# Attention and top-2 experts on one core: the first expert's tokens transposed on TensorE, gating cut at each hand-over, first weights split on GpSimd, zero fills issued by ScalarE

## The chip, the cores and the metric

One core of a Trainium2 chip runs the whole program. The metric is device time in microseconds (us) of that one core, as the median of several runs. A profile of one further execution shows what each engine did: TensorE (PE, with its weight loads PEld), VectorE (DVE), ScalarE (ACT), GpSimd (POOL) and the issuing engine SyncE (SP).

## What is computed

Linear attention without a softmax, a norm for each head, and then a layer of eight experts of which each token uses two. Cut to what matters:

```python
kv  = einsum('bhsd,bhse->bhde', k, v)          # 8 batches, 8 heads, 576 tokens, width 64
out = einsum('bhsd,bhde->bhse', q, kv)
x   = out / sqrt(mean(out*out, -1) + 1e-6) * g_norm      # 4608 tokens x 512
noisy = x @ w_gate + log1p(exp(x @ w_noise)) * noise
top2  = the two largest of 8;  weight = softmax over the two
for e in range(8):                             # w1[e] 512x1024, w2[e] 1024x512
    for k in range(2):
        m = top2[:, k] == e
        y[m] += weight[m, k] * (relu(x[m] @ w1[e]) @ w2[e])
```

## The kernel before

**Two stages that overlap.** The front stage computes 36 tiles of 128 tokens, nine for every two batches. `prep(b)` makes the 64x64 matrices of a batch (PE L539, then copies and small products by ACT L544, PE L549, ACT L552, PE L558, ACT L561, all through the tile `kvt` and into `kvw`). `tile_mm` multiplies the queries of one tile with it (PE L571, into the tile `big`). `advance(t)` is a hand-written pipeline: ACT copies `big` into `o` (L579, two `big` buffers), every second tile ACT squares it (`sq`, L586), DVE sums (`ss`, L588), ACT takes Ln and Exp of that sum one tile later (L592, L593), POOL scales tokens and logits one tile after that (`lg`, `x`, L602 and L606), DVE sums the logits (`zl`, L611), and ACT's queue writes the tokens to DRAM (`xs`, L615). Every engine takes its instructions in the order in which the program emits them: an instruction that waits holds all behind it on that engine.

**Gating in four chunks.** After tiles 10, 18, 28 and 36 a chunk is routed: `gating` turns logits into a choice of two experts and their weights, on DVE, ACT (L139, L140, L154) and POOL (L142, L143, L167) in turn, and PE counts the choices (L174). `onehots` and `place` (L302 to L315) make the list of an expert's tokens, and `finish` (L323) reads it out. These are generators: `yield n` gives the front stage n turns of `pump` before they go on; `pump` is called three times for each tile.

**Experts in units.** Expert 0 has five units of two tiles of tokens, here called units 0 to 4; the other experts have units of four, four and two. A unit's tokens are fetched by an indirect DMA on POOL's queue (`gather`, L357, tile `xg`), cut into a high and a low f16 half by ACT and POOL (`halves`, L364 and L365, tile `xh`), transposed by DMA (`xpose`, L377, tile `xT`; ACT's queue issues it for units 0 to 2, SP's for all others), multiplied by the first weights (`l1`, PE L416, relu by ACT L421 and DVE L422 into `hT`), by the second (`l2`, PE L460, ACT L481 into `y`), and added into the output by an indirect DMA that accumulates (`scatter`, POOL L394). Units 0, 1 and 2 are ready before the front stage ends: `fill_early` gives PE one piece of them per tile, so that l1 of unit 0 stands between the last tiles. The rest of unit 0 and units 1 and 2 follow the last tile.

**Weights.** Each expert's weights are scaled and cut into f16 halves. For expert 0 (`first_weights`, two steps per tile) DVE makes the low half straight from the f32 weights (L255, L257) while ACT makes the high one (L253).

**Zero fill.** The output has to be zero before the first scatter. Six DMAs of 1536 KB each (`clear`, L385) on SP's queue do that, emitted at tiles 30 to 35. The first scatter waits for all six.

Of the kernel before, what the change touches and what calls it, by code (L numbers as in the profile page):

```python
# [31 lines left out]
CHUNKS = (10, 18, 28, 36)  # L32
SL, W1 = 2, 2
KT, KV2 = 14, 0
XW, PY = 2, 5
LAG = 2
KC, KR, KQ, KX, KO = 5, 1, 4, 3, 3
GY = 5
WY, YH = 4, 4
YG, YX = 7, 7  # L40
KW0, KW1, KW = 100, 10, 8
MARKS = {10: 2, 18: 4, 28: 6}
EARLY = len(MARKS)
# [8 lines left out]
def attention_moe(ctx: ExitStack, tc: tile.TileContext, kvm, kvr, qt, gn, wgn, noise, w1, w2, out):  # L52
# [79 lines left out]
    def gating(a, b):  # L132
        n = b - a
        s = slice(a, b)
        w = rout.tile([P, n, E], F32, name="gt_w", bufs=2)
        nl = rout.tile([P, n, E], F32, name="gt_nl", bufs=2)
        V.scalar_tensor_tensor(w, zl[:, s, 8:16], -1.0, zl[:, s, 8:16], op0=OP.mult, op1=OP.max)
        V.tensor_scalar(nl, zl[:, s, 8:16], 1.0 / XS, 0.0, op0=OP.mult, op1=OP.max)
        A.activation(w, w, AF.Exp, scale=1.0 / XS)  # L139
        A.activation(w, w, AF.Ln, bias=1.0)  # L140
        yield 1
        G.tensor_tensor(w, w, nl, OP.add)  # L142
        G.tensor_tensor(w, w, nz[:, s], OP.mult)  # L143
        yield 1
        V.scalar_tensor_tensor(nl, zl[:, s, 0:8], 1.0 / XS, w, op0=OP.mult, op1=OP.add)
        mx = rout.tile([P, n, 8], F32, name="gt_mx", bufs=2)
        ix = rout.tile([P, n, 8], U32, name="gt_ix", bufs=2)
        for i in range(n):
            V.max(mx[:, i], nl[:, i])
        for i in range(n):  # L150
            V.max_index(ix[:, i], mx[:, i], nl[:, i])
        d = rout.tile([P, n, 4], F32, name="gt_d", bufs=2)
        V.tensor_tensor(d[:, :, 0:1], mx[:, :, 1:2], mx[:, :, 0:1], OP.subtract)
        A.activation(d[:, :, 1:2], d[:, :, 0:1], AF.Exp)  # L154
        ixf = rout.tile([P, n, 2], F32, name="gt_ixf", bufs=2)
        V.tensor_copy(ixf, ix[:, :, 0:2])
        yield 1
        oh = rout.tile([P, 2, n, E], F32, name="gt_oh", bufs=1)
        j8 = jf[:, None, 0:E].to_broadcast([P, n, E])
        for k in range(2):  # L160
            V.tensor_tensor(oh[:, k], j8, ixf[:, :, k:k + 1].to_broadcast([P, n, E]), OP.is_equal)
        V.tensor_scalar(d[:, :, 2:3], d[:, :, 1:2], 1.0, 1e-9, op0=OP.add, op1=OP.add)
        sel = rout.tile([P, n, E], BF, name="gt_sel", bufs=2)
        V.tensor_tensor(sel, oh[:, 0], oh[:, 1], OP.add)
        V.reciprocal(d[:, :, 2:3], d[:, :, 2:3])
        yield 1
        G.tensor_tensor(d[:, :, 3:4], d[:, :, 1:2], d[:, :, 2:3], OP.mult)  # L167
        for k in range(2):
            G.tensor_tensor(oh[:, k], oh[:, k], d[:, :, 2 + k:3 + k].to_broadcast([P, n, E]), OP.mult)
        G.tensor_tensor(ge[:, s], oh[:, 0], oh[:, 1], OP.add)  # L170
        yield GY
        for i in range(n):
            m = NT - a - i
            T.matmul(R[:, a + i + 1:, :], ones, sel[:, i:i + 1, :].to_broadcast([P, m, E]),  # L174
                     start=False, stop=False, skip_group_check=True)
        T.matmul(R[:, s, :], before, sel, start=False, stop=True, skip_group_check=True)
        V.tensor_copy(vals[:, 2, s], ge[:, s])
        yield 1
        vi = rout.tile([P, 2, n, E], I32, name="gt_vi", bufs=1)
        V.scalar_tensor_tensor(vi[:, 0], sel, -OFF, R[:, s, :], op0=OP.mult, op1=OP.add)  # L180
        G.tensor_tensor(w, ge[:, s], vals[:, 2, s], OP.subtract)
        if a:
            V.tensor_scalar(vi[:, 0, :, 0:1], vi[:, 0, :, 0:1], corr, None, op0=OP.add)
        if b in MARKS:
            gap = rout.tile([P, 1], F32, name="gap")
            V.tensor_tensor(gap, R[:, b, 0:1], corr, OP.add)
            V.tensor_scalar(gap, gap, -1.0, float(MARKS[b] * P), op0=OP.mult, op1=OP.add)
            V.tensor_scalar(gap, gap, 0.0, None, op0=OP.max)
            V.tensor_tensor(corr, corr, gap, OP.add)
        V.tensor_scalar(vi[:, 1], vi[:, 0], P - 1, None, op0=OP.bitwise_and)  # L190
        V.tensor_copy(lnb[:, s], vi[:, 1])
        V.tensor_tensor(t128[:, s], vi[:, 0], vi[:, 1], OP.subtract)
        yield 1
        V.tensor_copy(vals[:, 3, s], w)
        G.tensor_tensor(vals[:, 4, s], w, vals[:, 3, s], OP.subtract)
        yield 1
# [99 lines left out]
    def onehots(e, a, b):  # L296
        s = slice(a, b)
        n = b - a
        oa = lists.tile([P, n, P], BF, name="oa")
        ot = lists.tile([P, n, CAP], BF, name="ot")  # L300
        ob = lists.tile([P, n, 5, CAP], BF, name="ob")
        V.tensor_tensor(oa, jb[:, None, :].to_broadcast([P, n, P]),  # L302
                        lnb[:, s, e:e + 1].to_broadcast([P, n, P]), OP.is_equal)
        yield 1
        V.tensor_tensor(ot, tb10[:, None, :].to_broadcast([P, n, CAP]),
                        t128[:, s, e:e + 1].to_broadcast([P, n, CAP]), OP.is_equal)
        V.tensor_tensor(ob, ot[:, :, None, :].to_broadcast([P, n, 5, CAP]),
                        vals[:, :, s, e:e + 1].rearrange("p v n o -> p n v o").to_broadcast([P, n, 5, CAP]), OP.mult)
        return oa, ob
# [58 lines left out]
    def xpose(u):  # L368
        e, tiles, tail = units[u]
        if u < EARLY:  # L370
            if not u:
                late["xT"] = moe_a.tile([P, 8, 512], F16, name="xT")
            x = late["xT"][:, :, u % 2 * 256:(u % 2 + 1) * 256]
        else:
            x = (moe_a if (u - EARLY) % 2 else late["moe"]).tile([P, 8, 512], F16, name="xT")
        for i, t in enumerate(tiles):
            (A if u < EARLY else SP).dma_start_transpose(x[:, :, i * P:(i + 1) * P], XG[u, t])  # L377
        XT[u] = x

    outs = deque()  # L380
    zeroed = []
    ov = out[CAP * P:].rearrange("(p r) d -> p r d", p=P)

    def clear(r, n):
        zeroed.append(SP.dma_start(ov[:, r:r + n], zrow[:, None, :].to_broadcast([P, n, DM])).ins)  # L385

    tick = rout.tile([1, 1], F32, name="tick")
    SC = {e: [] for e in range(-1, E)}
# [99 lines left out]
    def drain(gen):  # L488
        for _ in gen:
            pass  # L490

    def moe_early(u):
        while "c" not in WT[0]:
            yield 1
        finish(0, M0, slice(2 * u, 2 * u + 2))
        yield 1
        gather(u)
        yield YG
        halves(u)
        yield YH  # L500
        xpose(u)
        yield YX
        while 0 not in loaded:
            yield 1
        early.extend([l1(u), l2(u)])

    early = deque()
# [3 lines left out]
    with tc.tile_pool(name="p1", bufs=2) as p1, tc.tile_pool(name="ps1", bufs=1, space=PSUM) as ps1:  # L511
# [148 lines left out]
        def fill_early():  # L660
            while early:
                try:
                    next(early[0])
                    if front[0] >= NT:
                        scatter()
                    return
                except StopIteration:
                    early.popleft()

        def first_weights():  # L670
            yield from weights(0, wts_a, V, SL)
            loaded.add(0)

        w0 = first_weights()
# [10 lines left out]
        for b in range(B):  # L685
# [7 lines left out]
            for args in per[b]:  # L693
                t = front[0] = args[0]
                tile_mm(*args)
                keep_warm(KW if t < KT else KV2)
                next(steps, None)
                if args[1] + args[4] < P:
                    next(steps, None)
                    continue  # L700
                pump()
                advance(t)
                next(steps, None)
                if t - LAG in CHUNKS:
                    side.append([1, chunk(CHUNKS.index(t - LAG))])
                pump()
                if t >= W1:
                    next(w0, None)
                    next(w0, None)
                fill_early()  # L710
                pump()
                if t >= NT - 6:
                    clear(6 * (t - NT + 6), 6)
            drain(steps)
        for t in range(NT, NT + 4):
            front[0] = t
# [3 lines left out]
                side.append([1, chunk(CHUNKS.index(t - LAG))])  # L720
            pump()
            fill_early()
    drain(w0)
    after = ExitStack()
    late["moe"] = after.enter_context(tc.tile_pool(name="moe_b", bufs=1))
# [4 lines left out]
    late["ps"] = ctx.enter_context(tc.tile_pool(name="psb", bufs=4, space=PSUM))  # L730
    psl = ctx.enter_context(tc.tile_pool(name="psl", bufs=1, space=PSUM))
    bg = deque()
    AHEAD = {0: gather, 8: halves, 15: xpose}
    hold = [0]

    def prepare(e):
# [55 lines left out]
    for u in (EARLY, EARLY + 1)[:1 + (GB > 4)]:  # L792
        for _ in range(XW):
            fill_early()
            fill()
        halves(u)
        fill_early()
        xpose(u)
    while early:
        fill_early()  # L800
        for _ in range(FE):
# [1 line left out]
    for u in range(EARLY, len(units) + 1):  # L803
        if u < len(units):
# [14 lines left out]
            if tiles[0] == 0 and e + 1 < E:  # L819
                bg.append(locate(e + 1))  # L820
                bg.append(prepare(e + 1))
            todo = deque([halves, xpose] if u + 1 < len(units) and u + 1 not in XT else ())
            while tail and todo:
                fill()
                todo.popleft()(u + 1)
# [94 lines left out]
```

## Time and profile before

| What | Value |
|---|---|
| Median of 3 runs | 981.3 us (980.8 to 986.57) |
| The profiled execution | 986.19 us, of which the span from first to last instruction is 984.3 us |
| PE busy | 906.2 us, 92% of the span |
| DVE, ACT, POOL busy | 460.2, 318.4, 380.9 us |
| PE busy from 0 to 50, 50 to 100, 100 to 150, 150 to 200 us | 46.17, 36.28, 35.54, 39.17 us |
| Granted PE clock in those four | 0.95, 0.74, 0.80, 0.90 |

Times within the profile count from the start of the span. A row of the timeline gives start, duration, engine, line, operation and tiles, and in brackets how long the engine had been idle before it and what ended that. The granted clock is the share of full speed at which the throttle let TensorE run.

### The profile page before, as it was taken

The numbers are of one execution on the slowest core, as the hardware profiler recorded it, in microseconds if no ns is written. First come the engines' busy times: TensorE is split into PE (matmuls) and PEld (weight loads), VectorE is DVE, ScalarE is ACT, GpSimd is POOL, SyncE is SP. The second block draws the span as 40 slices with busy tenths as digits, with TensorE's granted clock in tenths as the row PEclk, the third lists the DMA queues.
The fourth block names the chain that finished last, engine by engine and source line by source line (L and its number), as shares of the span: only waits on it lengthen the run. The fifth ranks groups of instructions, "written<-read, shape, count | busy, mean of one in ns | idle before, by whom it ended". The sixth has DMA issues, their size and how long they took to land.

```text
span 984.3 us, 15681 instructions
## 1 busy us (share of the span) xinstructions
PE 906.2 (92%) x6356; PEld 508.8 (52%) x6356; DVE 460.2 (47%) x933; ACT 318.4 (32%) x511; POOL 380.9 (39%) x414
## 2 busy tenths in 40 slices
PE   9986585999999999999999999999999989999994
PEld 8875473567444544464445344464444434644452
DVE  1678465555747343823563355534373456211110
ACT  1564343224334231323232332333243224222111
POOL 0445453554533352334244144325334553142122
PEclk9985697999999999999999899999999999999998
DMA  8998899655854873476259454637258644462224
GB/s 329 340 390 342 182 392 290 174 108 87 253 97 99 146 172 57 99 158 155 61 107 172 109 108 109 142 85 161 44 143 162 147 105 58 48 114 45 44 37 56
DMA packets 133898, 145.89 MB, mean 148 GB/s; under 512 B 90000, under 2 KB 90128, under 8 KB 133776
## 3 DMA queue, kind: packets, MB, share of 16 engines
q1 hardware_dynamic: 104624, 91.16, 33.4%
q0 software_dynamic: 17920, 41.95, 22.9%
q10 hardware_dynamic: 11232, 11.01, 3.8%
q8 instruction: 93, 1.52, 0.7%
q14 instruction: 29, 0.24, 0.1%
HBM read 83.02 MB, written 40.11 MB: 125 GB/s over the span
## 4 chain that ended last, share of the span: by engine, by line
PE 56%; DVE 5%; issue 2%; ACT 1%; POOL 1%; POOLq 0%; ACTq 0%
PE pp L460 31%; PE pp L416 24%; DVE mx L219 2%; DVE hT L422 1%; ACT hT L421 1%; POOL out_rows L394 1%; PE M L315 0%; PE pp L230 0%; DVE la L330 0%; DVE la L327 0%; DVE la L329 0%; DVE la L326 0%; POOLq L916 0%; DVE idx L328 0%; DVE row L331 0%
## 5 line engine op out<-in xcount | busy, mean ns | idle before, releaser
L460 PE MATMUL pp<-w2h,hT 128*128 128x512 f16 x1200 | 364.6, 381 | 9.5 <-ACT hT L421 5.6
L416 PE MATMUL pp<-xT,w1h 128*128 128x512 f16 (+5 forms) x1600 | 362.4, 323 | 4.3 <-issue 3.6
L394 POOL DMA_INDIRECT out_rows<-y,row x80 | 130.6, 1633 | 416.8 <-ACT y L481 413.2
L460 PEld LDWEIGHTS <-hT 128*128 128x128 f16 x1800 | 175.4, 98 | 221.4 <-issue 11.4
L422 DVE SCALAR_TENSOR_TENSOR hT<-pp,hT 128x512 f16<-128x512 f32 x160 | 107.0, 686 | 379.3 <-ACT hT L421 369.8
L416 PE MATMUL pp<-xT,w1l 128*128 128x512 f16 (+5 forms) x800 | 253.5, 323 | 0.0
L460 PE MATMUL pp<-w2l,hT 128*128 128x512 f16 x600 | 228.6, 381 | 0.0
L416 PEld LDWEIGHTS <-w1h 128*128 128x128 f16 x1600 | 149.0, 98 | 109.0 <-issue 4.3
L421 ACT ACTIVATE hT<-pp 128x512 f16<-128x512 f32 x160 | 92.0, 596 | 260.2 <-PE pp L416 230.5
L481 ACT ACTIVATE y<-pp,gate 128x512 f32<-128x512 f32 x80 | 54.0, 686 | 266.8 <-PE pp L460 235.4
L365 POOL TENSOR_TENSOR xh<-xg,xh 128x512 f16<-128x512 f32 x80 | 102.7, 1446 | 43.1 <-ACT xh L364 43.1
L416 PEld LDWEIGHTS <-w1l 128*128 128x128 f16 x800 | 78.6, 98 | 54.7
L357 POOL DMA_INDIRECT xg<-xs,idx x80 | 81.8, 1022 | 30.4 <-issue 21.3
L219 DVE TENSOR_REDUCE mx<-rw 128x1 f32<-128x1024 f32 x64 | 74.3, 1209 | 2.2 <-DMA rw<-w 2.2
L571 PE MATMUL big<-kvw,qt 64*128 64x80 f32 (+1 forms) x640 | 49.2, 301 | 20.2 <-ACT kvw L561 12.6
L571 PEld LDWEIGHTS big<-kvw,qt 64*128 64x128 f32 (+1 forms) x640 | 42.6, 203 | 26.2 <-ACT kvw L561 13.5
L364 ACT ACTIVATE xh<-xg 128x512 f16<-128x512 f32 x80 | 46.8, 623 | 19.9 <-DMA xg<-xs,idx 18.1
L302 DVE TENSOR_TENSOR oa<-jb,lnb 128x1152 bf16<-128x1152 bf16 (+2 forms) x32 | 48.2, 1507 | 0.0
L588 DVE TENSOR_REDUCE ss<-sq 128x16 f32<-128x1024 f32 x18 | 21.9, 1215 | 43.2 <-ACT sq L586 43.2
L602 POOL TENSOR_TENSOR lg<-o,ss 128x256 f32<-128x256 f32 x18 | 16.1, 895 | 63.6 <-DVE ss L596 60.4
L393 POOL MEMSET tick<- 1x1 f32 x80 | 39.3, 492 | 0.0
L606 POOL TENSOR_TENSOR x<-o,ss 128x512 f32<-128x512 f32 x36 | 38.6, 1090 | 0.0
(131 smaller groups left out, 564.1 us busy)
## 6 DMA issues: line engine op xcount, KB each, us to landing
rw<-w SPq DMA_DIRECT2D x64, 512.0 KB
kvc<-kvm SPq DMA_DIRECT2D x32, 512.0 KB
xs<-x ACTq DMA_DIRECT2D x18, 512.0 KB
out_rows<-zrow SPq DMA_DIRECT2D x6, 1536.0 KB
qt<-qt SPq DMA_DIRECT2D x8, 640.0 KB
qt<-qt SPq DMA_DIRECT2D x8, 512.0 KB
kvr<-kvr SPq DMA_DIRECT2D x4, 512.0 KB
xg<-xs,idx POOLq DMA_INDIRECT x80
```

The costliest lines, as they stand in the source:

```text
L219: V.tensor_reduce(mx[:, c:c + 1], src[:, c], axis=AX.X, op=OP.max, apply_absolute_value=True)
L302: V.tensor_tensor(oa, jb[:, None, :].to_broadcast([P, n, P]), lnb[:, s, e:e + 1].to_broadcast([P, n, P]), OP.is_equal)
L357: G.indirect_dma_start(out=x, out_offset=None, in_=src, in_offset=bass.IndirectOffsetOnAxis(ap=LI[e][:, t:t + 1], axis=0))
L364: A.activation(x[:, 0], XG[u, t], AF.Copy)
L365: G.tensor_tensor(x[:, 1], XG[u, t], x[:, 0], OP.subtract)
L394: d = G.indirect_dma_start(out=out, out_offset=bass.IndirectOffsetOnAxis(ap=LS[e][:, t:t + 1], axis=0), in_=y, in_offset=None, compute_op= ...
L416: T.matmul(ps[:, f % ps.shape[1], 0:n], w[wn][:, c, f * P:(f + 1) * P], x[:, xo + c, 0:n], start=(c == 0 and k == 0), stop=(c == HP - 1 an ...
L421: A.activation(h[:, 0, f:f + nf, 0:n], ps, AF.Relu)
L422: V.scalar_tensor_tensor(h[:, 1, f:f + nf, 0:n], ps, 0.0, h[:, 0, f:f + nf, 0:n], op0=OP.max, op1=OP.subtract)
L460: T.matmul(ps, h[:, hk, f, i * P:(i + 1) * P], w[wn][:, f], start=(f == 0 and k == 0), stop=(f == 7 and k == 2))
L481: A.activation(y, ps, AF.Copy, scale=LG[e][:, t:t + 1])
L571: T.matmul(TL[t][r0:r0 + n, h, hp * 80:(hp + 1) * 80], q[r, hp, s0 - o:s0 - o + n], KVW[b][r, hp], start=True, stop=True, skip_group_check ...
```

## The change

It has four parts and a set of new turn counts.

1. `xpose` becomes a generator. For units 0 to 4 it no longer issues DMA transposes: PE transposes each gathered f32 tile of 128x512 in four pieces of 128x128 into PSUM, ACT copies the result as f16 (the high half) and DVE subtracts that copy from PSUM (the low half). `halves` is not called for these five units. The other units keep their path.
2. `gating` and `onehots` yield where one engine hands over to the next, and ACT's Exp of the two best logits comes before DVE's `max_index` instead of behind it.
3. `first_weights` is called with POOL in DVE's place. That takes the other branch of `split`, which stood there before: ACT scales a quarter of the weights in place and then copies it to f16, two instructions for one, and POOL subtracts.
4. `clear` is issued by ACT instead of SP, at tiles 32 to 35 and at the two turns behind the last tile; the first scatter is emitted only when all six have been.

```diff
-XW, PY = 2, 5
+XW, PY = 2, 6
-GY = 5
-WY, YH = 4, 4
-YG, YX = 7, 7
+GY = 3
+WY = 4
+YG, YX = 5, 2
...
         V.tensor_scalar(nl, zl[:, s, 8:16], 1.0 / XS, 0.0, op0=OP.mult, op1=OP.max)
+        yield 1
         A.activation(w, w, AF.Exp, scale=1.0 / XS)
...
         G.tensor_tensor(w, w, nz[:, s], OP.mult)
-        yield 1
+        yield 2
         V.scalar_tensor_tensor(nl, zl[:, s, 0:8], 1.0 / XS, w, op0=OP.mult, op1=OP.add)
...
+        yield 1
+        A.activation(d[:, :, 1:2], d[:, :, 0:1], AF.Exp)
         for i in range(n):
             V.max_index(ix[:, i], mx[:, i], nl[:, i])
...
         for i, t in enumerate(tiles):
-            (A if u < EARLY else SP).dma_start_transpose(x[:, :, i * P:(i + 1) * P], XG[u, t])
+            if u > EARLY + 1:
+                SP.dma_start_transpose(x[:, :, i * P:(i + 1) * P], XG[u, t])
+            else:
+                ps = ps_tile([P, HP, P])
+                for c in range(HP):
+                    T.transpose(ps[:, c], XG[u, t][:, c * P:(c + 1) * P], ident)
+                yield YX
+                n = slice(i * P, (i + 1) * P)
+                A.activation(x[:, 0:HP, n], ps, AF.Copy)
+                V.tensor_tensor(x[:, HP:, n], ps, x[:, 0:HP, n], OP.subtract)
         XT[u] = x
+        yield YX
...
     def clear(r, n):
-        zeroed.append(SP.dma_start(ov[:, r:r + n], zrow[:, None, :].to_broadcast([P, n, DM])).ins)
+        zeroed.append(A.dma_start(ov[:, r:r + n], zrow[:, None, :].to_broadcast([P, n, DM])).ins)
...
         gather(u)
         yield YG
-        halves(u)
-        yield YH
-        xpose(u)
-        yield YX
         while 0 not in loaded:
             yield 1
+        yield from xpose(u)
         early.extend([l1(u), l2(u)])
...
-                    if front[0] >= NT:
+                    if len(zeroed) == 6:
                         scatter()
...
-            yield from weights(0, wts_a, V, SL)
+            yield from weights(0, wts_a, G, SL)
...
-                if t >= NT - 6:
-                    clear(6 * (t - NT + 6), 6)
+                if t >= NT - 4:
+                    clear(6 * (t - NT + 4), 6)
...
+            if t < NT + 2:
+                clear(6 * (t - NT + 4), 6)
...
-        halves(u)
-        fill_early()
-        xpose(u)
+        while u > EARLY and len(early) > 1:
+            fill_early()
+        for _ in xpose(u):
+            fill_early()
```

**ACT, from the second transpose stop to tile 34.** `o` is the copy of a tile, `xs<-x` the write of two tiles of tokens. Before:

```order
L561 ACTIVATE kvw<-kvt 128x4x16
L377 DMA_TRANSPOSE xT<-xh 128x8x128 x2
L154 ACTIVATE gt_d<-gt_d 128x10
L615 DMA xs<-x 128x2x512
L579 ACTIVATE o<-big 128x640
L586 ACTIVATE sq<-o 128x1024
```

The changed kernel, from the copy of tile 32 on:

```order
L589 ACTIVATE o<-big 128x640
L398 DMA out_rows<-zrow 128x6x512
L625 DMA xs<-x 128x2x512
L589 ACTIVATE o<-big 128x640
L596 ACTIVATE sq<-o 128x1024
L398 DMA out_rows<-zrow 128x6x512
L602 ACTIVATE ss<-ss,eps 128x16
L603 ACTIVATE ss<-ss 128x16
L589 ACTIVATE o<-big 128x640
L398 DMA out_rows<-zrow 128x6x512
```

The DMA transposes are gone from ACT, and the first three fills stand behind the copies of tiles 32, 33 (with its square) and 34; three more follow behind tile 35 and at the next two turns.

**POOL, the first scatter and what stands behind it,** with the semaphores that each waits for (those named DMAHW are of DMAs that SP or ACT issued). Before:

```order
L394 DMA out_rows<-y,row_135 5888x512 [waits DMAHW3_49,DMAHW2_49,DMAHW7_49,DMAHW1_49,Activation_49]
L357 DMA xg<-xs,idx_127 128x512 [waits DVE_49]
L357 DMA xg<-xs,idx_127 128x512
L142 TENSOR_TENSOR gt_w<-gt_w,gt_nl 128x64 [waits DVE_49,Activation_49]
L143 TENSOR_TENSOR gt_w<-gt_w,nz 128x64 [waits Pool_49]
```

The changed kernel:

```order
L407 DMA out_rows<-y,row_135 5888x512 [waits DMAHW3_49,DMAHW5_49,DMAHW1_49,DMAHW6_49,DMAHW0_49,Activation_49]
L360 DMA xg<-xs,idx_127 128x512 [waits DVE_49]
L360 DMA xg<-xs,idx_127 128x512 [waits DMASW0_49,PE_49]
L143 TENSOR_TENSOR gt_w<-gt_w,gt_nl 128x64 [waits Activation_49]
L144 TENSOR_TENSOR gt_w<-gt_w,nz 128x64 [waits Pool_49]
```

The order is the same: scatter, the two gathers of unit 2, the gating of the last chunk. What moved is the fills that the scatter waits for: from SP's queue, ahead of the last tiles, to ACT's, between them and behind them.

**PE, in the middle of unit 1's l1** (`RM<-gt_sel` counts the last chunk's choices). Before:

```order
L416 LDWEIGHTS w1l
L416 MATMUL pp<-xT,w1l 128x256
L174 LDWEIGHTS ones
L174 MATMUL RM<-gt_sel,ones 128x64
L174 LDWEIGHTS ones
```

The changed kernel:

```order
L429 LDWEIGHTS w1l
L429 MATMUL pp<-xT,w1l 128x256
L385 MATMUL pp<-ident,xg 128x128 x4
L429 LDWEIGHTS w1h
L429 MATMUL pp<-xT,w1h 128x256
```

Half of unit 1's l1 now has the transposes of unit 2's first tile behind it, and the counting comes 36 matmuls later, behind those of the second tile; the half is 48 of the unit's 96 matmuls in both.

More of the change, by code (lines that the diff above doesn't have):

```diff
@@ L149, in gating @@
             V.max(mx[:, i], nl[:, i])
+        d = rout.tile([P, n, 4], F32, name="gt_d", bufs=2)
+        V.tensor_tensor(d[:, :, 0:1], mx[:, :, 1:2], mx[:, :, 0:1], OP.subtract)
+        yield 1
+        A.activation(d[:, :, 1:2], d[:, :, 0:1], AF.Exp)
         for i in range(n):
             V.max_index(ix[:, i], mx[:, i], nl[:, i])
-        d = rout.tile([P, n, 4], F32, name="gt_d", bufs=2)
-        V.tensor_tensor(d[:, :, 0:1], mx[:, :, 1:2], mx[:, :, 0:1], OP.subtract)
-        A.activation(d[:, :, 1:2], d[:, :, 0:1], AF.Exp)
         ixf = rout.tile([P, n, 2], F32, name="gt_ixf", bufs=2)
@@ L161, in gating @@
             V.tensor_tensor(oh[:, k], j8, ixf[:, :, k:k + 1].to_broadcast([P, n, E]), OP.is_equal)
-        V.tensor_scalar(d[:, :, 2:3], d[:, :, 1:2], 1.0, 1e-9, op0=OP.add, op1=OP.add)
         sel = rout.tile([P, n, E], BF, name="gt_sel", bufs=2)
         V.tensor_tensor(sel, oh[:, 0], oh[:, 1], OP.add)
+        V.tensor_scalar(d[:, :, 2:3], d[:, :, 1:2], 1.0, 1e-9, op0=OP.add, op1=OP.add)
         V.reciprocal(d[:, :, 2:3], d[:, :, 2:3])
@@ L306, in onehots @@
                         t128[:, s, e:e + 1].to_broadcast([P, n, CAP]), OP.is_equal)
+        yield 1
         V.tensor_tensor(ob, ot[:, :, None, :].to_broadcast([P, n, 5, CAP]),
@@ L732, in attention_moe @@
     bg = deque()
-    AHEAD = {0: gather, 8: halves, 15: xpose}
+    turn = lambda u: drain(xpose(u))
+    AHEAD = {0: gather, 8: halves, 15: turn}
     hold = [0]
@@ L821, in attention_moe @@
                 bg.append(prepare(e + 1))
-            todo = deque([halves, xpose] if u + 1 < len(units) and u + 1 not in XT else ())
+            todo = deque([halves, turn] if u + 1 < len(units) and u + 1 not in XT else ())
             while tail and todo:
```

## The prediction, made before the changed kernel ran

> **What bounds the kernel now.** I read the busy shares first, then the waits of PE, then the timelines of PE and ACT around the longest of them. The head of the page:
>
> ```profile
> span 984.3 us, 15681 instructions
> PE 906.2 (92%) x6356; PEld 508.8 (52%) x6356; DVE 460.2 (47%) x933; ACT 318.4 (32%) x511; POOL 380.9 (39%) x414
> ```
>
> PE is idle for 984.3 − 906.2 = 78 us. All else it must do, and the change takes no matmul away; so what can be won lies in those 78 us, and what is lost is a new wait of PE. The waits of PE name the engine that ended them (total, times, longest):
>
> ```profile
> PE big L571 <- ACT kvw L561: 12.6, 4, 7.6
> PE kvt L558 <- ACT kvT L552: 12.0, 6, 8.3
> PE big L571 <- ACT o L579: 7.5, 2, 7.0
> ```
>
> Each has one long instance, all in the front stage, and the timeline of PE places them (a fourth, shorter one comes later):
>
> ```profile
> 101.53 1.33 PE L571 MATMUL big<-kvw,qt 64*64 64x80 f32 x16 [7.62 <-ACT kvw L561]
> 119.69 1.04 PE L558 MATMUL kvt<-gw,kvT 64*64 64x16 f32 x16 [8.28 <-ACT kvT L552]
> 154.89 2.00 PE L571 MATMUL big<-kvw,qt 64*128 64x80 f32 x16 [7.01 <-ACT o L579]
> 192.08 0.39 PE L460 MATMUL pp<-w2h,hT 128*128 128x512 f16 x1 [1.95 <-ACT hT L421]
> ```
>
> What ACT did meanwhile is in its own timeline (ACTq is its queue issuing a DMA):
>
> ```profile
> 93.63 0.26 ACT L139 ACTIVATE gt_w<-gt_w 128x64 f32<-128x64 f32 x1 [1.95 <-DVE gt_w L137]
> ...
> 99.09 0.22 ACT L154 ACTIVATE gt_d<-gt_d 128x8 f32<-128x8 f32 x1 [2.84 <-DVE gt_d L153]
> ...
> 108.84 9.13 ACTq L377 DMA_TRANSPOSE xT<-xh  x2
> 118.01 0.31 ACT L592 ACTIVATE ss<-ss,eps 128x16 f32<-128x16 f32 x1 [8.18 <-issue]
> ...
> 119.06 0.58 ACT L552 ACTIVATE kvT<-kvt 64x512 f32<-64x512 f32 x1
> ...
> 145.37 7.21 ACTq L377 DMA_TRANSPOSE xT<-xh  x1
> ...
> 157.67 1.28 ACT L579 ACTIVATE o<-big 128x640 f32<-128x640 f32 x2
> ```
>
> The second and the third stall of PE are ACT held by issuing DMA transposes, 9.13 and 7.21 us; the first is a chain of small waits and copies on ACT. From the last row, the copies of tiles 32 and 33, I measure what the front stage gains: its 157.67 is the mark "tile 32" below.
>
> **The transposes leave ACT's queue.** Without them the second stall ends when ACT has its other inputs. The sum that L592 waits for, and PE's `kvt`, came from
>
> ```profile
> 109.87 1.22 DVE L588 TENSOR_REDUCE ss<-sq 128x16 f32<-128x1024 f32 x1 [4.41 <-ACT sq L586]
> 109.73 0.63 PE L549 MATMUL kvt<-ident,kvw 128*64 128x128 f32 x4
> ```
>
> that is, at 111.1 and 110.4. From L592 to L552 ACT took 119.06 − 118.01 = 1.05; 111.1 + 1.05 is about 112.2, so kvT comes 6.9 us earlier. The third stall: `big` is full, so without the issue all 7.0 us go. The first stays as long, as far as I can see: two waits of 1.95 and 2.84 leave (the new yields put other work between), but the split below adds four ACT copies there, 4 × 1.135 = 4.5. I take 0, between −3 and +3.
>
> The clock after a stall adds a little. Twelve matmuls of l1 behind the second stall, and the same twelve later:
>
> ```profile
> 123.71 0.61 PE L416 MATMUL pp<-xT,w1h 128*128 128x256 f16 x2 [0.61 <-DMA xT<-xh]
> ...
> 126.38 1.17 PE L571 MATMUL big<-kvw,qt 64*128 64x80 f32 x16
> ...
> 131.38 0.39 PE L416 MATMUL pp<-xT,w1h 128*128 128x256 f16 x2
> ...
> 132.80 0.45 PE L571 MATMUL big<-kvw,qt 64*128 64x80 f32 x4
> ```
>
> 2.67 against 1.42 us: 1.2 for each of two stalls that go, 2.4.
>
> PE's new work: no transpose of tokens on PE is in this trace, but four f32 transposes (the L549 row above) took 0.63 us. A tile needs four, five units have ten tiles: 6.3 us, of which 2.5 come before tile 32 (units 0 and 1), 1.3 with unit 2, 2.5 behind. The pieces are of 128 partitions and not 64, so a bound above is twice that; below, they could fall into idle time and cost nothing. I take 0.63. The Trainium skill, *VectorE: DVE Perf Modes*, section "The three transpose paths", has 390 ns for one 128x128 transpose on TensorE; by that page the ten tiles would cost an estimated 15.6 us and the result would lie some 9 us higher. The four in the row took 0.16 each, so I stay with the row.
>
> The evacuation changes hands one for one, and is hidden:
>
> ```profile
> L365 POOL TENSOR_TENSOR xh<-xg,xh 128x512 f16<-128x512 f32 x80 | 102.7, 1446 | 43.1 <-ACT xh L364 43.1
> L421 ACT ACTIVATE hT<-pp 128x512 f16<-128x512 f32 x160 | 92.0, 596 | 260.2 <-PE pp L416 230.5
> L422 DVE SCALAR_TENSOR_TENSOR hT<-pp,hT 128x512 f16<-128x512 f32 x160 | 107.0, 686 | 379.3 <-ACT hT L421 369.8
> ```
>
> ACT's copy from PSUM is priced like L421 (0.60, against 0.63 for the L364 that it replaces), DVE's subtraction like L422 (0.69), and POOL loses 1.45 a tile. DVE has room for ten times 0.69 over 150 us; uncovered it would be 6.9 us.
>
> **First weights on POOL, and the yields.** In the busy stretch of the front stage (sum us, with instructions, of PE, PEld, DVE, ACT, POOL; then granted clock, DMA share, GB/s), and the two halves by line:
>
> ```profile
> 50.00:100.00 50.00, 36.28 (x549) 32.15 (x545) 41.16 (x141) 27.65 (x52) 25.35 (x30) 0.74 0.92 355
> L253 ACT ACTIVATE w2h<-rw,sc 128x1024 f16<-128x1024 f32 x12 | 13.0, 1135 | 0.4 <-DVE sc L236 0.4
> L255 DVE SCALAR_TENSOR_TENSOR w2l<-rw,sc,w2h 128x1024 f16<-128x1024 f32 x9 | 11.2, 1281 | 3.2 <-ACT w2h L253 3.2
> ```
>
> DVE, 41.16 of 50 us, loses eight L255 of about 1.28 = 10 us; ACT, 27.65 of 50, gains eight copies of 1.135 = 9; POOL, 25.35, gains at most 8 × 2.9 (twice L365's 1.446, which has half the elements) = 23. No engine comes over its 50 us, POOL by little. So this part should cost nothing in sum; it moves work from DVE, for which PE has no long wait, to ACT, for which it has, and that is in the first stall's +3; if DVE was the hidden limit, up to 10 us more are won. That is a rival below. PE's l1 pieces of unit 0 come earlier too: eight instead of six chunks of about 1.5 us before tile 32, so +3 there and nothing in total.
>
> Sum to tile 32: −6.9 − 7.0 − 2.4 + 2.5 = −13.8 won, and the +3.0 of work moved ahead of it: 157.7 − 10.8 = 146.9, with the first stall's ±3.
>
> **The fills.** Here is the price. Now they start at 123 on SP; a view of DMA issues and the stretch until they are in:
>
> ```profile
> 123.07 20.14 SPq L385 DMA_DIRECT2D out_rows<-zrow  x6
> out_rows<-zrow SPq DMA_DIRECT2D x6, 1536.0 KB
> xs<-x ACTq DMA_DIRECT2D x18, 512.0 KB
> 123.00:159.00 36.00, 25.54 (x328) 21.16 (x326) 18.11 (x71) 14.36 (x31) 13.78 (x20) 0.83 1.06 364
> ```
>
> The DMA engines are full there (share 1.06), 364 GB/s. In the changed kernel the first fill is issued behind tile 32's copy, at about 147.6. Six fills of 1536 KB and three writes of tokens of 512 KB that stand on ACT's queue between them are 9.4 + 1.6 = 11.0 MB: 30 us at 364 GB/s. SP's load of the next expert's weights lies in the same time (2.1 MB): 36 us if all of it goes ahead. I take 33, so the last fill is in at about 180.6. The Trainium skill, *DMA: Bandwidth & Descriptors*, section "Queues, rings and completion order", says that each DMA engine takes turns between its queues packet by packet; by that the load of weights shares the time and the upper figure is the nearer. The trace has no such pair of queues alone, so it moves no term.
>
> The first scatter, which now runs at once, must wait for that, and POOL is in order:
>
> ```profile
> 173.89 1.63 POOL L394 DMA_INDIRECT out_rows<-y,row  x1 [0.16 <-issue]
> 175.82 1.00 POOL L357 DMA_INDIRECT xg<-xs,idx  x1 [0.31 <-DVE gt_nl L138]
> ```
>
> Behind it are unit 2's two gathers and the last chunk's gating. Who waits for the gathers: ACT's copy of the second tile, and in the changed kernel PE itself, since unit 2's transposes stand in the middle of unit 1's l1:
>
> ```profile
> 183.30 0.63 ACT L364 ACTIVATE xh<-xg 128x512 f16<-128x512 f32 x1 [1.04 <-DMA xg<-xs,idx]
> 182.14 0.38 PE L416 MATMUL pp<-xT,w1h 128*128 128x256 f16 x2
> ...
> 187.38 0.38 PE L460 MATMUL pp<-w2h,hT 128*128 128x512 f16 x1
> ```
>
> The second tile was in 183.30 − 173.89 = 9.4 after the scatter began, the first, one gather earlier, about 1.3 sooner: 8.1. So PE gets unit 2's first tile at 180.6 + 8.1 = 188.7. It has reached the place (182.14 now, half of unit 1's l1 done) some 14 us sooner than now, at about 168: it waits about 20. From there the other half of l1 is 187.38 − 182.14 = 5.2, say 5.4, two tiles' transposes 1.3, and 1.2 for the clock after so long a stop: l1 of unit 1 ends at 196.6, where it ended at 187.4. **+9.2.** Behind that the 1.95 stall at 192.08 (again ACT, issuing two transposes) is gone with its small change, −2.3, and units 3 and 4 are transposed by PE, +2.5: +9.4, in whole numbers 9.
>
> PE is the chain that ends last, full from there, so the end moves by as much. The profiled execution took 986.19 (its span 984.3) and lies 4.9 above the median of 981.3; by the terms, 995 for it and **990 for the median**.
>
> **Rivals.** *One, the other side: the front stage gains twice as much.* If DVE is the real limit, its 10 us come off on top, and every stall with them. Tile 32 at 137.5 or sooner is the point at which it decides: fills in at 171, unit 2's tile at 179, l1 of unit 1 at 187, level with now, and 192.08's 2.3 pays for the last transposes: 981, nothing lost. For it: DVE's 41.16 of 50 us and the two gating waits on DVE. Against: no long stall names DVE.
>
> *Two, the fills don't bind.* They would have to be in by about 160, 11.0 MB in 12 us, over 900 GB/s; the page's row of throughput,
>
> ```profile
> GB/s 329 340 390 342 182 392 290 174 108 87 253 97 99 146 172 57 99 158 155 61 107 172 109 108 109 142 85 161 44 143 162 147 105 58 48 114 45 44 37 56
> ```
>
> never exceeds 392. It can only be if the scatter doesn't wait as its list of semaphores says, or if the front gains very much more. Then 13.8 and 2.3 are won and 3.8 of transposes (units 2 to 4) are paid: 981.3 − 12.3 = 969.
>
> *Three, ACT is held by issuing fills.* SP needed
>
> ```profile
> L385 SPq DMA_DIRECT2D out_rows<-zrow x6: 427/2644/5880, 123.1 to 141.4; - x6
> ```
>
> 0.43, 2.64 and up to 5.88 us (least, middle, most) to issue one. On ACT that time stands ahead of the copies and relus of the last tiles. Four such of 2.64 are 10.6 us. They delay the front's end by less than PE's 20 us of new waiting, so mostly they hide; but three token writes behind them are late too, and the last fill is issued later: some 5 more, 995.
>
> *Four, the stalls only move, so that the change doesn't do what it says:* loads from DRAM (share 0.92 in 50 to 100) set the pace, tile 32 comes at 153 and everything 6 later: 996. Against it:
>
> ```profile
> SPq L517 <- PE kvt L539: 29.8, 13, 16.9
> ```
>
> SP waits for PE to free the load buffers, not the other way round.
>
> **How the numbers follow.** The forecast 0.42, rival one 0.25, two 0.10, three 0.13, four 0.10. The forecast's own range is 984 to 1000: −3 from the first stall, −3 from 30 us for the fills; +3, +3, and +6 from transposes at twice their price, which are unlikely all together. The given range is 972 to 1000, which leaves out most of rival two and the tails. One per cent either way, 971.5 and 991.1, is about what a measurement can tell here: faster is most of rival two and a fifth of one, 0.15; slower is nearly half of the forecast and three quarters of rivals three and four, 0.36; within 1% the rest, 0.49.
>
> **What would show it.** In the changed profile: no DMA transposes on ACT, PE's stalls of 8.28 and 7.01 gone, and tile 32's copy at 147 ± 4 (at 137, rival one; at 153, rival four). The fills in at 177 to 184, POOL's first scatter just behind them with a wait of some 15 to 20 us, and one stall of PE of about 20 us in unit 1's l1 that ends with unit 2's gathered tile. Four transposes at 0.6 to 0.7 us. Fills on ACT's queue with 2 to 6 us of issue each would be rival three. The prediction is wrong if the scatter does not wait, or if PE finds work while it does.

## The result, and the profile after

The changed kernel takes 1010.7 us (median of 4 runs, 1007.43 to 1013.53) against 982.4 for the kernel before (981.3 in the three runs that stood ahead of the prediction): a ratio of 1.028, with a 95% interval of 1.023 to 1.033. The forecast was 990, with a range of 972 to 1000. The loss is about three times as large as forecast (28 us against 9). The head of the profile:

```profile
span 1011.8 us, 15757 instructions
PE 917.8 (91%) x6396; PEld 516.3 (51%) x6396; DVE 445.8 (44%) x935; ACT 327.6 (32%) x519; POOL 383.6 (38%) x412
```

The span is 27.5 us longer. PE works 11.6 us more: 8.1 us are the 40 transposes, and the rest goes with a mean granted clock of 0.949 instead of 0.961. It is idle for 94 us instead of 78. Its three largest waits, in total, times and longest:

```profile
PE pp L385 <- DMA xg<-xs,idx: 24.8, 3, 20.9
PE pp L232 <- DVE dg L228: 14.9, 6, 9.5
PE kvt L568 <- ACT kvT L562: 8.5, 4, 5.7
```

The first line is the wait that the prediction was made of. The second was in no rival. First the part that came as forecast, on ACT's, POOL's and PE's timelines:

```profile
147.55 0.38 ACTq L398 DMA_DIRECT2D out_rows<-zrow  x1
147.66 0.69 ACT L589 ACTIVATE o<-big 128x640 f32<-128x640 f32 x1
```

```profile
179.93 1.63 POOL L407 DMA_INDIRECT out_rows<-y,row  x1 [15.87 <-issue]
181.86 1.00 POOL L360 DMA_INDIRECT xg<-xs,idx  x1 [0.30 <-issue]
```

```profile
189.01 1.11 PE L385 MATMUL pp<-ident,xg 128*128 128x128 f32 x4 [20.85 <-DMA xg<-xs,idx]
...
197.10 0.38 PE L473 MATMUL pp<-w2h,hT 128*128 128x512 f16 x1
```

Tile 32 is copied at 147.66 (forecast 146.9), the first scatter starts at 179.93 (180.6), unit 2's first tile is there at 189.01 (188.7) after a stop of 20.85 (20), and unit 1's l1 ends at 197.10 (196.6), where it ended at 187.38 before. Up to here the kernel is 9.7 us behind, as forecast. Now the rest, in the order of time on PE (`M<-ob` is one of four steps that make the list of the second expert's tokens, here the last; `pp<-dg` is the step by which the scale of a weight matrix is found, once for each of its two matrices; the last row is its first l1 matmul):

```profile
219.37 0.68 PE L385 MATMUL pp<-ident,xg 128*128 128x128 f32 x4 [2.37 <-DMA xg<-xs,idx]
...
249.08 0.39 PE L318 MATMUL M<-ob,oa 128*128 128x50 bf16 x9 [3.27 <-DVE ob L310]
...
265.35 0.46 PE L232 MATMUL pp<-dg,onef 128*128 128x128 f32 x2 [2.65 <-DVE dg L228]
280.49 0.76 PE L232 MATMUL pp<-dg,onef 128*128 128x128 f32 x2 [9.50 <-DVE dg L228]
281.04 1.06 PE L429 MATMUL pp<-xT,w1h 128*128 128x512 f16 x2
```

Before, the same two steps of the weights waited for nothing, and the second expert began 26.6 us sooner:

```profile
232.77 0.39 PE L230 MATMUL pp<-dg,onef 128*128 128x128 f32 x2
...
254.23 0.38 PE L230 MATMUL pp<-dg,onef 128*128 128x128 f32 x2
254.45 0.59 PE L416 MATMUL pp<-xT,w1h 128*128 128x512 f16 x2
```

So the loss grows from 9.7 at the end of unit 1's l1 to 26.6 at the start of the second expert, and hardly after that (27.5 at the end). DVE shows why the scale is late: it looks for the largest weights (L221) only behind the copy of the finished list (L327). Then it has four such reductions to do, a matmul of PE to wait for, four low halves to make and four more reductions, for the second matrix, whose `pp<-dg` stands ahead of the second expert's l1 on PE's queue.

```profile
249.51 0.21 DVE L327 COPY m<-M 128x50 f32<-128x50 f32 x1 [0.48 <-PE M L318]
...
251.08 2.34 DVE L221 TENSOR_REDUCE mx<-rw 128x1 f32<-128x1024 f32 x2
```

Before, it began 26 us sooner:

```profile
225.14 2.34 DVE L219 TENSOR_REDUCE mx<-rw 128x1 f32<-128x1024 f32 x2
```

The order of the program says the same without times. On PE's queue before, all four steps of the second expert's list stand ahead of unit 3's l1, and the first weight scale stands 72 of 96 matmuls into it. In the changed kernel the first step of the list stands 12 matmuls into unit 3's l1, the last behind the 96, and both scales later still. This work is emitted by `fill`, one turn at a time, between PE's pieces of units 1 and 2. The change uses these pieces up without `fill`: in the longer turns of gating before the lists are done, and in the two new loops (`while u > EARLY ...: fill_early()` and `for _ in xpose(u): fill_early()`).

Three explanations are put to the test. **Theory A:** two losses that have nothing to do with each other, the fills that the scatter waits for, and the second expert's preparation that is emitted too late. **Rival B:** one loss; the lists are late because gating stands behind the scatter on POOL, so undoing the fills brings all back. **Rival C:** the loss is PE's own, transposes and the slow clock after stalls.

### The profile page after: what moved, and what is told of

Its sections match the earlier page's. It is cut to its first block, busy times and chain, and to the rows that moved or that the text cites. A ratio compares the mean times of both kernels' runs of the same rounds, so it can differ in the third digit from the quotient of the medians.

```text
span 1011.8 us, 15757 instructions
## 1 busy us (share of the span) xinstructions
PE 917.8 (91%) x6396; PEld 516.3 (51%) x6396; DVE 445.8 (44%) x935; ACT 327.6 (32%) x519; POOL 383.6 (38%) x412
## 5 line engine op out<-in xcount | busy, mean ns | idle before, releaser
L429 PE MATMUL pp<-xT,w1h 128*128 128x512 f16 (+5 forms) x1600 | 368.5, 327 | 8.1 <-issue 7.0
L429 PE MATMUL pp<-xT,w1l 128*128 128x512 f16 (+5 forms) x800 | 256.8, 327 | 0.0
L368 POOL TENSOR_TENSOR xh<-xg,xh 128x512 f16<-128x512 f32 x70 | 89.9, 1360 | 47.5 <-ACT xh L367 47.4
L221 DVE TENSOR_REDUCE mx<-rw 128x1 f32<-128x1024 f32 x64 | 74.5, 1208 | 1.7 <-DMA rw<-w 1.7
L367 ACT ACTIVATE xh<-xg 128x512 f16<-128x512 f32 x70 | 41.1, 624 | 21.1 <-DMA xg<-xs,idx 17.4
L257 DVE SCALAR_TENSOR_TENSOR w1l<-rw,sc,w1h 128x1024 f16<-128x1024 f32 x21 | 27.3, 1333 | 25.8 <-ACT w1h L255 25.8
```

The lines of the kernel that those rows point to most:

```text
L221: V.tensor_reduce(mx[:, c:c + 1], src[:, c], axis=AX.X, op=OP.max, apply_absolute_value=True)
L367: A.activation(x[:, 0], XG[u, t], AF.Copy)
L368: G.tensor_tensor(x[:, 1], XG[u, t], x[:, 0], OP.subtract)
L429: T.matmul(ps[:, f % ps.shape[1], 0:n], w[wn][:, c, f * P:(f + 1) * P], x[:, xo + c, 0:n], start=(c == 0 and k == 0), stop=(c == HP - 1 an ...
```

## The experiments

Each set ran beside the kernel before on one chip; ratios are to that one.

### The two losses apart

The fills on SP again, and with them the old condition of the first scatter (e1_fills_sp, cut to the fills):

```diff
-        zeroed.append(A.dma_start(ov[:, r:r + n], ...
+        zeroed.append(SP.dma_start(ov[:, r:r + n], ...
-                if t >= NT - 4:
-                    clear(6 * (t - NT + 4), 6)
+                if t >= NT - 6:
+                    clear(6 * (t - NT + 6), 6)
...
-            if t < NT + 2:
-                clear(6 * (t - NT + 4), 6)
```

> The changed kernel with the six zero fills on SP again, at tiles 30 to 35 as before; all else is the change. Theory A (two separate losses: about 10 us by the scatter that waits for the fills, up to unit 3, and about 13 to 17 us because the preparation of the second expert's weights stands later in the program): the 20.85 us stall of PE goes, the first half of the loss comes back, the second stays: the first l1 matmul of the second expert at about 265 to 270 instead of 281, and 996 to 1001 in all. Rival B (the late second expert is only the late gating of the last chunk, which stands behind the scatter on POOL): all comes back and the front stage's gain shows, 970 to 980. Rival C (slow clock and the new transposes are the loss): stays above 1003.

998.4 us, ratio 1.013 (1.008 to 1.019). The scatter starts without a wait, and the other loss is untouched:

```profile
164.78 1.62 POOL L407 DMA_INDIRECT out_rows<-y,row  x1 [0.16 <-issue]
```

```profile
264.01 0.77 PE L232 MATMUL pp<-dg,onef 128*128 128x128 f32 x2 [9.50 <-DVE dg L228]
264.57 1.06 PE L429 MATMUL pp<-xT,w1h 128*128 128x512 f16 x2
```

Gating is early here and the 9.50 is still there to the hundredth: rival B falls. The second expert begins at 264.57, 16.5 sooner than in the changed kernel and a little sooner than the 265 to 270 expected.

The background work spread over the pieces (e2_background; four turns, where the last loop had two):

```diff
         while u > EARLY and len(early) > 1:
             fill_early()
+            for _ in range(4):
+                fill()
         for _ in xpose(u):
             fill_early()
+            for _ in range(4):
+                fill()
     while early:
         fill_early()
-        for _ in range(FE):
+        for _ in range(4):
             fill()
```

> The changed kernel with four turns of background work (lists and weights of the second expert) behind each piece of PE work in the two loops that have none, and four instead of two in the loop behind them, so that the counting of the second expert's tokens and its first weight scale stand about where they stood before on PE's queue. Fills stay on ACT. Theory A: the 20.85 us stall stays, the 9.50 us wait for the weight scale goes, 994 to 1000. Rival B (the lists wait for the late gating on DVE whatever their place): within 4 us of the changed kernel, 1007 to 1013.

1001.9 us, ratio 1.018 (1.013 to 1.024): a gain, though 2 us above the 994 to 1000 expected. The wait for the fills stays, the 9.50 goes; the longest wait for the scale is now 5.7:

```profile
PE pp L385 <- DMA xg<-xs,idx: 24.2, 3, 20.7
PE pp L232 <- DVE dg L228: 7.9, 4, 5.7
```

Both edits (e3_both):

> Both edits: fills on SP at tiles 30 to 35 and the background work paced as before. Theory A: both losses go and what the front stage gained shows, 968 to 980 (front stage about 10 to 14 us sooner, 6 us of new transposes paid). Rival C (slow clock and the new transposes): above 985.

989.1 us, ratio 1.006 (1.003 to 1.009). The two gains nearly add up (1.5% and 1.0% alone, 2.2% together), which theory A asks for, but the time misses the expected 968 to 980 and lies where rival C was expected, above 985. The timeline shows a new wait:

```profile
225.60 0.80 PE L232 MATMUL pp<-dg,onef 128*128 128x128 f32 x2 [5.72 <-DVE dg L228]
```

Four turns each are too many. The scale now stands on PE's queue right ahead of unit 3's l1, sooner than DVE can have it. The next run, again with both edits, puts it back to where it was, 72 matmuls into that l1 (e5_pace; the same three loops with three, three and four turns, shown against e3):

```diff
-            for _ in range(4):
+            for _ in range(3):
                 fill()
```

> As the run with both edits (fills on SP, background work behind the pieces), but with fewer turns (three, three, four), so that the first weight scale of the second expert stands 72 instead of 0 matmuls into unit 3's l1 on PE's queue, where it stood before. Theory A (the place of that step decides, too late cost 14 us, too early left a wait of 5.72): the 5.72 goes and nothing like 9.50 comes, second expert's first l1 at 248 to 253, 978 to 985. Rival B (the list work of DVE for the second expert is late by itself): as the run with both edits, 987 to 991.

980.8 us, ratio 0.997 (0.994 to 1.000), within the expectation. Neither step of the weights waits any more:

```profile
227.38 0.46 PE L232 MATMUL pp<-dg,onef 128*128 128x128 f32 x2
...
249.02 0.38 PE L232 MATMUL pp<-dg,onef 128*128 128x128 f32 x2
249.24 0.59 PE L429 MATMUL pp<-xT,w1h 128*128 128x512 f16 x2
```

At the second expert's first matmul the 26.6 us divide as follows. From the kernel before, 254.45, to e5, 249.24, is the front's gain, 5.2. From e5 to e1, 264.57, is the late preparation, 15.3. From e1 to the changed kernel, 281.04, are the fills, 16.5. Such steps add up whatever their causes; what gives each its cause is that e1 and e5 differ in the pacing alone, and e1 and the changed kernel in the fills alone. PE's waits agree for the preparation: from 195 us to the second expert, e1 waits 3.3 us for the list and 12.3 for the two scales, together 15.6, and e5 has none of these waits. From that matmul to the end, the profiles of the kernel before, the changed kernel and all eleven runs take between 727 and 735 us, so that at the end of the program the same steps are less exact: 12.5 us of span for the fills, 18.2 for the preparation.

Rival C can't be the cause of the loss: e5 has all the transposes, PE is busy for 5.6 us more in it than before (911.8 against 906.2), and it is not slower than before.

### The fills by themselves

In the kernel before, only the fills moved (e4_before_fills_act; the lines of e1 the other way round, and the scatter as in the change):

> The kernel before, with only the fills moved: issued by ACT at tiles 32 to 35 and at the two turns behind. Theory A: the first scatter, at 173.9 before, waits for the fills until about 190 to 195, unit 2's second tile comes by as much later, and l1 of unit 2 starts 8 to 15 us later: 988 to 997. If the wait were hidden here: within 3 us of the kernel before, 979 to 985.

989.3 us, ratio 1.006 (1.003 to 1.009). The time is as expected, and the mechanism is there, on POOL and on PE, which waits for the gating behind the scatter:

```profile
181.06 1.62 POOL L394 DMA_INDIRECT out_rows<-y,row  x1 [15.08 <-DMA out_rows<-zrow]
```

```profile
186.37 0.42 PE L174 MATMUL RM<-gt_sel,ones 128*128 128x64 bf16 x8 [13.00 <-DVE gt_sel L164]
```

But the scatter came at 181, not at 190 to 195, since the front stage became 10.7 us faster (tile 32's copy at 146.93 instead of 157.67), by the fills' absence alone. Two of ACT's transpose issues show it. Before, with the fills' traffic:

```profile
142.85 2.43 ACTq L377 DMA_TRANSPOSE xT<-xh  x1
```

The next one, a row of the prediction, took 7.21. The same two without the fills:

```profile
138.93 1.26 ACTq L377 DMA_TRANSPOSE xT<-xh  x1
140.28 1.30 ACTq L377 DMA_TRANSPOSE xT<-xh  x1
```

So the third stall of the kernel before, 7.01 us, needed the fills as well as the transposes: it is gone here, with the transposes still on ACT's queue, and gone in e1, with the fills still ahead of the last tiles.

The paced kernel with the fills on ACT, but earlier (e6_fills_early):

```diff
-                if t >= NT - 4:
-                    clear(6 * (t - NT + 4), 6)
+                if 26 <= t < 32:
+                    clear(6 * (t - 26), 6)
...
-            if t < NT + 2:
-                clear(6 * (t - NT + 4), 6)
```

> As the paced kernel, but the fills are issued by ACT at tiles 26 to 31, from about 125 us, where the changed kernel used only 0.43 of the DMA engines' time between 125 and 150. Theory A (fills on ACT are harmful only because they start at 147): the first scatter does not wait, and the second tile of unit 1 comes as early as in the changed kernel; within 3 us of the paced kernel, either way. Rival three of the prediction (ACT held by issuing): ACT spends 10 us or more in issuing, the copies of tiles 27 to 33 come later, and it is 4 us or more slower than the paced kernel.

981.4 us, ratio 0.999 (0.996 to 1.002), the same as e5. ACT spends 0.38 to 2.98 us in issuing a fill, and tile 32 comes at 151.34 against 151.81. So in this kernel it is not ACT's queue that hurts but the time at which the fills start. One expectation failed: the gather for unit 1 still meets the fills' traffic, and PE waits for it 3.53 us (4.79 in e5, 1.53 in the changed kernel).

### What the front stage gained, and from what

The changed kernel with the split on DVE (e7_split_dve):

```diff
-            yield from weights(0, wts_a, G, SL)
+            yield from weights(0, wts_a, V, SL)
```

> The changed kernel with the first weights split on DVE and ACT again as before. The prediction's term for this part is 0: copy of tile 32 within 3 us of the changed kernel's 147.66. If the move to POOL was what freed the front (rival one), tile 32 comes 5 us or more later. The time as the changed kernel, 1005 to 1015, unless the later places of the second expert's work move too.

1003.5 us, ratio 1.020 (1.013 to 1.026); tile 32 is copied 13.7 us sooner:

```profile
133.99 0.69 ACT L589 ACTIVATE o<-big 128x640 f32<-128x640 f32 x1
```

Neither of the two cases expected came, and the time is below its range as well. My term of 0 was wrong by all of the 13.7. PE's stalls near 100 in the changed kernel and the same two in this one:

```profile
98.10 0.92 PE L568 MATMUL kvt<-gw,kvT 64*64 64x16 f32 x13 [5.74 <-ACT kvT L562]
102.80 1.33 PE L581 MATMUL big<-kvw,qt 64*64 64x80 f32 x16 [2.52 <-ACT kvw L571]
```

```profile
89.83 0.93 PE L568 MATMUL kvt<-gw,kvT 64*64 64x16 f32 x13 [1.97 <-ACT kvT L562]
94.47 1.33 PE L581 MATMUL big<-kvw,qt 64*64 64x80 f32 x16 [2.47 <-ACT kvw L571]
```

They also come 8 us sooner. The wait for the fills takes nothing of the 13.7: it starts sooner too, PE stops for 20.89 us, and unit 2's first tile is there at 175.37, 13.6 sooner. At the second expert's first matmul (272.77) 8.3 are left, and 7 reach the end; which of the waits between takes the 5.3 was not tested.

The DMA transposes again, with `halves` as before but emitted later than before, behind the first weights (e8_dma_transposes):

```diff
-            if u > EARLY + 1:
-                SP.dma_start_transpose(x[:, :, i * P:(i + 1) * P], XG[u, t])
-            else:
+            (A if u < EARLY else SP).dma_start_transpose(x[:, :, i * P:(i + 1) * P], XG[u, t])
...
+        halves(u)
+        yield 4
         yield from xpose(u)
...
+        halves(u)
         while u > EARLY and len(early) > 1:
```

> The changed kernel with units 0 to 4 cut into halves and transposed by DMA again (issued by ACT for units 0 to 2, by SP for 3 and 4); yields, split on POOL and fills on ACT stay. The prediction's terms say that these transposes held ACT for 14 us of PE's stalls: the 7 to 8 us stalls come back, tile 32's copy at 155 to 160 instead of 147.66, the first fill and so the first scatter as much later, 1010 to 1022. If the new yields or the split made the front faster, tile 32 stays below 151.

1015.2 us, ratio 1.032 (1.025 to 1.039). Tile 32 comes at 159.45, 11.8 us later than in the changed kernel, both as expected. But the two stalls of 7 to 8 us don't come back. There is one, of another kind:

```profile
125.56 0.61 PE L429 MATMUL pp<-xT,w1h 128*128 128x256 f16 x2 [12.78 <-DMA xT<-xh]
```

Here PE waits for the transposed tokens of unit 0 themselves. Issuing them held ACT for 6.88 us at 111.09; the next pair, with no fills under way, for 2.65.

Last, the paced kernel with the split on DVE (e9_paced_dve, three turns in all three loops), the same with the early fills on ACT (e10_early_dve), and e9 with the old gating (e11_old_gating; its yields, the place of the Exp and the order of its steps as before; three, two and two turns, where the added yield in the lists stays, so that the scale keeps its place about):

> The paced kernel (fills on SP at tiles 30 to 35, background work behind the pieces, three turns each) with the first weights split on DVE and ACT as before. Theory D (the split on POOL with ACT's extra copy cost the front stage 12 to 14 us, hidden in the changed kernel by what the yields and the transposes won): tile 32's copy at 133 to 140, and since the fills start behind SP's last load, 10 us sooner too, the whole comes through: 966 to 973. Rival E (the front's gain is lost again at the scatter or the gathers, as in the changed kernel): 976 to 983.

> As the one before, with the fills issued by ACT at tiles 26 to 31. Theory D: within 3 us of it, 965 to 974. If issuing six fills holds ACT at tiles that are now closer together: tile 32's copy 3 us or more later and the time by as much.

> As the paced kernel with the split on DVE, but with gating's own yields and order as before (the added yield in the lists stays; the turns of the background work are set so that the second expert's first weight scale stands where it did). If the yields are what shortened the front stage's first stall (7.62 before, 1.97 in the changed kernel with the split on DVE): PE's stall near 100 is back at 5 us or more, tile 32's copy 3 to 6 us later, 970 to 979. If they only move waits about: within 2 us.

e9: 969.7 us, ratio 0.983 (0.979 to 0.988). e10: 970.8, ratio 0.985 (0.981 to 0.988), tile 32 at 141.20; both are within what was expected. e11: 982.7, ratio 0.999 (0.996 to 1.003), slower than the 970 to 979 expected. e9 beats both kernels: 15 us below the one before, in that set 984.4. Its second expert begins at 241.23, 8 us ahead of e5:

```profile
141.60 0.69 ACT L589 ACTIVATE o<-big 128x640 f32<-128x640 f32 x1
```

```profile
127.01 1.09 PE L385 MATMUL pp<-ident,xg 128*128 128x128 f32 x4 [4.98 <-DMA xg<-xs,idx]
...
241.23 0.59 PE L429 MATMUL pp<-xT,w1h 128*128 128x512 f16 x2
```

Tile 32 comes at 141.60, later than the 133 to 140 expected: a gather meets the fills, which now start at 109. In e11 the first stall of the kernel before is back to the hundredth or so, and tile 32 comes 8.0 us later than in e9, more than the 3 to 6 expected; the second expert begins 12.5 later (253.68), and what the other 4.5 are stays open:

```profile
100.93 1.33 PE L579 MATMUL big<-kvw,qt 64*64 64x80 f32 x16 [7.63 <-ACT kvw L569]
```

```profile
149.58 0.69 ACT L587 ACTIVATE o<-big 128x640 f32<-128x640 f32 x1
```

## Why the prediction was wrong, point by point

**The step that failed** is the last of the sum: "PE is the chain that ends last, full from there, so the end moves by as much." The forecast's +9 held up to unit 1's l1 (9.7), but the loss was 26.6 at the second expert's start. In the kernel before, PE was full from there only because the second expert's preparation had been put between PE's pieces in time. I looked at what the change moves around the first scatter, and not at what it does to the background work that is emitted turn by turn behind it. That cost 15.3 us at the second expert's start (e1 against e5), in new waits of PE for the list and the scales, of which the longest was 9.50.

**The fills** were right in mechanism and nearly in size, point by point up to 197.10: from the first fill to the scatter 32.4 us (33 forecast), PE's stop 20.85 (about 20). That these steps also fell at the forecast times rests on tile 32's mark. As the price of the whole part, 16.5 us stand at the second expert (the changed kernel against e1).

**Tile 32 at 146.9 was right by luck.** The terms against the runs, each in the kernel where one edit was undone:

| Term | Forecast | Measured at tile 32's copy |
|---|---|---|
| Transposes off ACT's queue, with the clock and PE's own transposes | −13.8 | −11.8 (changed kernel against e8) |
| Gating's yields and order | within the first stall's 0 ± 3 | −8.0 (e9 against e11) |
| Split on POOL | within the same 0 ± 3 | +13.7 (changed kernel against e7), +10.2 (e5 against e9) |
| Fills away from the front | none | −3.8 (changed kernel against e1), −10.7 (e4 against the kernel before) |
| Unit 0's pieces earlier | +3.0 | not measured apart |
| Sum | −10.8 | −10.0 (changed kernel against the kernel before) |

Kernels that are the same up to there have this mark within 1.1 us of each other (147.66 in the changed kernel, 146.52 in e2; 151.48, 152.49 and 151.81 in e1, e3 and e5), so the differences in the table are well above that. Two terms of −8.0 and +13.7 us had been set to zero, and the fills' −3.8 had been left out; together these come to +1.9, and that is the luck. The first value of each row adds up to −9.9; but where a term was measured in two kernels the values differ by 3.5 and 6.9 us, so that such a sum is no proof.

The transposes' −11.8 is near its forecast, but by another wait. The forecast added up two stalls in which ACT was held by issuing; in e8, where the transposes are issued later than in the kernel before, the loss is one wait of PE, 12.78 for the transposed tokens, with ACT's 6.88 of issuing inside it. For the third stall the prediction named the transposes alone, and e4 removes it by moving the fills.

The split's price could partly have been read: the extra copies stand on ACT, in order, ahead of the copies that PE waits for. In the changed kernel four passes of the split (92.19 to 96.5) stand ahead of the copy of `kvT` at 97.47 for which PE waits 5.74 us; in e7 two do (86.08 to 88.2), and PE waits 1.97. I had counted 4.5 us of them once; that the rest of the 13.7 is the same at other batches, and the first weights' low half that comes later too, is argued and not shown.

**Rival one** (the front stage gains twice as much, since DVE is the real limit) was possible in size, as e7 shows with tile 32 at 133.99, but its mechanism was wrong: in e7 the split is back on DVE. Gating's yields and order brought 8.0 (e9 against e11), and relieving DVE cost more than it brought. **Rival two** (the fills don't bind) is out: the scatter waits 15.87 us, and 0.16 when only the fills are moved (e1). **Rival three** (ACT held by issuing) happened in small: the six issues took 0.38 to 1.52 us each, two writes of tokens 4.17 and 3.88, all of it inside the wait for the fills. **Rival four** (the stalls only move, tile 32 at 153) is out: tile 32 came at 147.66, and in e8, with the DMA transposes, at 159.45.

**The price of a transpose on PE** held nearly: four took between 0.60 and 1.11 us (the 1.11 at 189.01, behind the long stop), against the 0.63 taken, and all 40 took 8.1 against 6.3. The Trainium skill, *VectorE: DVE Perf Modes*, section "The three transpose paths", with its 390 ns for one, given for bf16, would make that an estimated 1.56 us for four. The f32 rows here are all below that.

**The chance for slower** by over 1% was 0.36. Every case of mine ended at 996 or sooner, and not one of them had a loss in the second expert's preparation.

## What to carry to other kernels

Where background work is emitted turn by turn between pieces of the main work, a change that adds turns or uses pieces up moves that work against the main engine; compare its place, counted in the main engine's instructions, before forecasting the time. Price a transfer that something must wait for by when it starts; which queue issues it mattered little here (e5 and e6, 980.8 and 981.4 us). When a forecast of a mark comes true, undo each term by itself before it is believed.

## What the runs showed of the hardware that I had not expected

With a fill of 9.4 MB under way, two issues of DMA transposes took 2.43 and 7.21 us on ACT's queue; with the fills moved away they took 1.26 and 1.30 (e4). The gathers on POOL's queue come later too: PE waited 4.73 us for one with the fills on SP (e1), 1.53 in the changed kernel, where none were under way, and both gathers were issued within 0.4 us of the same time (129.07 and 128.69):

```profile
137.96 1.09 PE L385 MATMUL pp<-ident,xg 128*128 128x128 f32 x4 [4.73 <-DMA xg<-xs,idx]
```

```profile
134.38 1.01 PE L385 MATMUL pp<-ident,xg 128*128 128x128 f32 x4 [1.53 <-DMA xg<-xs,idx]
```

The Trainium skill, *DMA: Bandwidth & Descriptors*, section "Queues, rings and completion order", says that the engines take turns between queues packet by packet. These rows fit sharing of that kind but don't show the turns themselves: a gather that is small by itself still came some 3 us late.

The split by groups of instructions (busy, then mean ns of one), in the changed kernel's first 300 us: GpSimd's subtraction of 128x1024 takes 2.13 us where VectorE made the same half in 1.28 (the L255 row of the prediction), and ScalarE's extra scaling in place takes 1.14 ahead of its copy.

```profile
L250 ACT ACTIVATE rw<-rw,sc 128x1024 f32<-128x1024 f32 x8 | 9.1, 1139 | 4.1 <-DVE sc L241 2.2 <-DVE sc L238 1.9
L248 POOL TENSOR_TENSOR w1l<-rw,w1h 128x1024 f16<-128x1024 f32 x4 | 8.5, 2130 | 4.3 <-ACT w1h L251 4.3
```
